# A linear-attention layer followed by a gated long convolution on one core: an order of 1,088 words laid anew

## The chip, the cores and the metric

The kernel runs on one core of a Trainium2 chip. The metric is the device time of one execution in microseconds; the runs of the kernel before took 159.25, 159.96 and 160.06 us, median 159.96. One further execution was profiled. A core has five engines that work through their own instruction lists: TensorE (PE, matmuls; its weight loads are shown as PEld), VectorE (DVE), ScalarE (ACT), GpSimd (POOL) and SyncE (SP), whose queue (SPq) starts the transfers (DMA).

## The reference

Two layers follow one another, over 4 batches, 8 heads, 768 steps and 48 channels in a head.

```python
state = np.zeros((B, H, D, D))
for t in range(S):
    y[:, :, t] = einsum('bhd,bhde->bhe', r_t, state + einsum('bhd,bhe->bhde', u * k_t, v_t))
    state = w_t[..., None] * state + einsum('bhd,bhe->bhde', k_t, v_t)
x = y laid out as (4, 768, 384)
x1, x2, x3 = split(x @ w_proj, 3)
x2_conv = irfft(rfft(x2, axis=1) * rfft(filter_fft, axis=0), n=768)
out = (x1 * x2_conv * x3) @ w_out
```

The first part is a recurrence with a decay w per step and channel, the second a circular convolution over the whole sequence, with a gate on either side.

## The kernel before, in words

The sequence of each batch is cut into 6 chunks of 128 steps, 24 chunks in all; chunk c belongs to batch c // 6. A chunk needs four loads (ldw, ldk, ldr, ldv, 192 KB each; six buffers of each kind). The logarithm of w (lw, ACT) is summed along the steps by two matmuls with triangular masks (cs with the step itself, ce without it), and exponentials of the sums (eq, en) scale r and k: q on the one side, kh on the other. These products can be made in two forms: ACT writes the exponential to SBUF and POOL multiplies (en and kh, eq and q), or ACT writes it back into its PSUM bank and DVE multiplies from there (enp and khp, eqp and qp). TensorE transposes both (tqk), a copy brings them back (tT, L231 or L232), their products are the scores (sc), and DVE masks them while it copies them from PSUM (mt, L560); in another form ACT copies (ma) and POOL masks (mm). Keys and values give the state (kv, then S on DVE, L589). The step's own term, with u, is a product rk of r and k, times u (rku), summed per head (cc) and multiplied onto v (vc); it is added either by a matmul with the identity in the word yb, after which a copy takes the result (xc), or by DVE (y, then xn). The chunk's output is transposed (yt) into xT, and the second half of a batch also makes sums and differences with the first half (sa, sb).

When these exist, the second layer of that batch can start: projections x2 (L682) of sums and differences, copied by ab; the forward transform f (L395, L402) with a matrix F of sines; products with the filter's transform T in the tables UA, UB and their sum P (da, db or X, ua, ub; pp); projections p1 and p3 (L651) with copies x1 and the gate g (or gc by ACT and gm); the inverse transforms i1, i2 (L722), a copy ec, sums and differences s and d (L744, L753), the gate product yy, the output matmul po (L764), its copy o and the store st. Batches overlap: chunks 6 to 11 are worked on while batch 0 is in its second layer.

At the start the kernel also makes its constants. POOL writes a ramp into the first row block of the tile filt (iota), DVE makes 384-wide angles from it (ang0 to ang2, L316, and one column, angn), and ACT takes the sines that are F, and the twelve factors rot (sin, L332 and L336, which needs another ACT table than the logarithms and exponentials; the table is changed back at its end, L337). The filter's load ldfilt (L346, 1,152 KB) overwrites the ramp, so it waits for the angle words. From the filter fs makes the sum of its two halves (L385) and fd the difference (L388); hf0 to hf5 transform them, and rot, which rsc scales (L340), weighs the results into T (ht on ACT, L420, and hr on DVE, L425). The transposed blocks of F for the inverse are mtr, mc and ms. The words z and zs are matmuls of zeros on TensorE whose result nobody reads, 512 or 128 columns wide, as many as the number behind the name says (L791, L796).

The order is written out in one string, ORDER, of 1,088 words. A word such as `P:hf0@3` names the engine (P TensorE, V VectorE, A ScalarE, G GpSimd, S SyncE), the operation with its arguments, and behind the @ the PSUM bank. Every engine works through its own words in the order of the string; semaphores follow from the data and from buffers that are used again. A word with an exclamation mark takes its turn: it also waits for the last VectorE word before it in the string whose operation stands in the set `shut`, as emit arranges it:

```python
if e == "V" and op in shut:
    last[0] = ins
if after and ins is not None and last[0] is not None:
    tc.add_manual_dep(ins.ins, last[0].ins.name, ...)
```

Here ins is what the operation's function returns, and some of these functions return nothing.

## Time and profile before

| what | value |
|---|---|
| runs | 159.25, 159.96, 160.06 us |
| the profiled execution | 159.13 us |
| its span, first to last instruction | 157.4 us |
| PE, DVE, ACT, POOL busy | 142.6, 136.6, 126.0, 111.0 us |
| mean granted TensorE clock | 0.966 |
| read from and written to HBM | 22.61 and 4.72 MB |

The span is the part of the device time that the profile sees. Busy times of matmuls are modelled from their starts, so a busy TensorE need not be at its peak. In a timeline row stand the start and the duration in us, the engine, the line of the kernel, the operation, output and inputs, and in brackets how long the engine was idle before, and for whom.

### The profile page before, as it was taken

The numbers are of one execution on the slowest core, as the hardware profiler recorded it, in microseconds if no ns is written. First come the engines' busy times: TensorE is split into PE (matmuls) and PEld (weight loads), VectorE is DVE, ScalarE is ACT, GpSimd is POOL, SyncE is SP. The second block draws the span as 40 slices with busy tenths as digits, with TensorE's granted clock in tenths as the row PEclk, the third lists the DMA queues.
The fourth block names the chain that finished last, engine by engine and source line by source line (L and its number), as shares of the span: only waits on it lengthen the run. The fifth ranks groups of instructions, "written<-read, shape, count | busy, mean of one in ns | idle before, by whom it ended". The sixth has DMA issues, their size and how long they took to land.

```text
span 157.4 us, 4146 instructions
## 1 busy us (share of the span) xinstructions
PE 142.6 (91%) x1541; PEld 92.8 (59%) x1544; DVE 136.6 (87%) x264; ACT 126.0 (80%) x261; POOL 111.0 (71%) x134
## 2 busy tenths in 40 slices
PE   6972499899899999999899999999999999999970
PEld 6441266667565667676566667676666767545530
DVE  5425978999999999999999989999999999998940
ACT  3795439999898999999898999999897887655541
POOL 7121728999999959899939994789699939283000
PEclk9997559999999999999999999999999999999999
DMA  5998989999996989999999899999945000000966
GB/s 102 203 277 184 215 170 201 209 251 191 236 210 145 265 160 213 186 203 218 179 252 189 158 205 196 187 226 216 218 138 200 0 4 2 0 0 4 329 240 233
DMA packets 105844, 27.60 MB, mean 175 GB/s; under 512 B 100320, under 2 KB 105824, under 8 KB 105824
## 3 DMA queue, kind: packets, MB, share of 16 engines
q1 hardware_dynamic: 105824, 27.34, 77.4%
q8 instruction: 12, 0.20, 0.5%
q14 instruction: 8, 0.07, 0.1%
HBM read 22.61 MB, written 4.72 MB: 174 GB/s over the span
## 4 chain that ended last, share of the span: by engine, by line
PE 58%; ACT 10%; DVE 8%; DMA 8%; POOL 5%; issue 5%; SPq 3%; ACTq 0%; DVEq 0%; POOLq 0%
PE p L651 13%; PE x L682 6%; PE po L764 6%; DMA ldk<-in_k_dram 5%; PE f L402 5%; PE tqk L540 4%; PE i L722 4%; PE sc L553 3%; PE f L395 3%; SPq L450 2%; DMA ldw<-in_w_dram 2%; PE y L606 2%; PE ce L466 2%; DVE rot L340 2%; ACT xT L231 2%
## 5 line engine op out<-in xcount | busy, mean ns | idle before, releaser
L651 PE MATMUL p<-xT,wproj 128*128 128x384 bf16 x144 | 29.0, 326 | 0.0
L521 POOL TENSOR_TENSOR rk<-ldr,ldk 128x384 bf16<-128x384 f32 x23 | 23.0, 1002 | 7.4 <-DMA ldk<-in_k_dram 3.1
L560 DVE TENSOR_TENSOR mt<-sc,mask_excl 128x1024 bf16<-128x1024 f32 x22 | 26.7, 1216 | 0.5 <-PE sc L553 0.4
L231 ACT ACTIVATE qkT<-tqk 128x1024 bf16<-128x1024 bf16 x21 | 21.6, 1027 | 2.4 <-PE tqk L540 1.7
L534 POOL TENSOR_TENSOR vc<-v,cc 128x384 bf16<-128x384 bf16 x24 | 19.8, 831 | 3.8 <-ACT v L231 1.5
L518 POOL TENSOR_TENSOR qk<-ldr,eq 128x384 bf16<-128x384 f32 x17 | 17.0, 1001 | 3.0 <-ACT eq L485 3.0
L651 PEld LDWEIGHTS <-wproj 128*128 128x128 bf16 x144 | 12.8, 98 | 7.3 <-DVE sd L641 0.3
L540 PE MATMUL tqk<-ident,qk 128*128 128x128 bf16 x192 | 15.4, 223 | 1.1 <-DVE qk L502 1.1
L682 PE MATMUL x<-wproj,sd 128*128 128x384 bf16 x72 | 15.0, 326 | 1.0 <-ACT ab L231 0.6
L524 POOL TENSOR_TENSOR rku<-rk,u_bc 128x384 bf16<-128x384 bf16 x15 | 13.7, 915 | 2.7 <-DVE y L756 1.5
L722 PE MATMUL i<-m_b,P 128*128 128x384 bf16 x72 | 15.0, 326 | 0.0
L764 PE MATMUL po<-wout,y 128*128 128x384 bf16 x72 | 14.5, 326 | 0.5 <-DVE y L756 0.3
L540 PEld LDWEIGHTS <-qk 128*128 128x128 bf16 x192 | 12.1, 99 | 4.6 <-DVE qk L502 1.7
L456 ACT ACTIVATE lg<-ldw 128x384 bf16<-128x384 f32 x24 | 12.6, 524 | 2.5 <-DMA ldw<-in_w_dram 2.5
L514 POOL TENSOR_TENSOR qk<-ldk,en 128x384 bf16<-128x384 f32 x12 | 12.0, 1002 | 2.4 <-ACT x L231 2.0
L231 ACT ACTIVATE ab<-x 128x384 bf16<-128x384 f32 x24 | 11.4, 495 | 2.5 <-PE x L682 2.3
L527 DVE TENSOR_REDUCE cc<-rku 128x8 f32<-128x384 bf16 x24 | 12.9, 541 | 0.0
L231 ACT ACTIVATE x<-p 128x384 bf16<-128x384 f32 x24 | 11.6, 501 | 0.7 <-PE p L651 0.7
L231 ACT ACTIVATE xT<-yt 128x384 bf16<-128x384 bf16 x23 | 11.0, 494 | 1.0 <-DVE sd L638 0.8
L589 DVE TENSOR_TENSOR S<-kv,eq 128x384 bf16<-128x384 f32 x20 | 11.0, 550 | 0.8 <-PE kv L581 0.7
L710 DVE TENSOR_TENSOR UA<-f,T 128x768 bf16<-128x768 f32 x11 | 10.4, 949 | 0.3 <-PE f L395 0.3
L677 POOL TENSOR_TENSOR g<-g,x 128x384 bf16<-128x384 bf16 x8 | 7.2, 913 | 4.7 <-DVE g L677 2.6
(137 smaller groups left out, 372.8 us busy)
## 6 DMA issues: line engine op xcount, KB each, us to landing
ldw<-in_w_dram SPq DMA_DIRECT2D x24, 192.0 KB, 3.7
ldr<-in_r_dram SPq DMA_DIRECT2D x24, 192.0 KB, 3.9
ldk<-in_k_dram SPq DMA_DIRECT2D x24, 192.0 KB, 3.9
ldv<-in_v_dram SPq DMA_DIRECT2D x24, 192.0 KB, 4.0
out_dram<-o SPq DMA_DIRECT2D x12, 192.0 KB, 2.2
out_dram<-filt SPq DMA_DIRECT2D x12, 192.0 KB, 2.1
...
filt<-in_moe_filter_fft_dram SPq DMA_DIRECT2D x1, 1152.0 KB, 8.4
```

The costliest lines, as they stand in the source:

```text
L231: return nc.scalar.activation(out=o, in_=i, func=AF.Copy)
L518: return two(e).tensor_mul(qk_b[c % 3][:, 0, :, 0:D], ld["r"][c % LD], eq)
L521: return two(e).tensor_mul(rk_b[c % 2], ld["r"][c % LD], ld["k"][c % LD])
L524: return two(e).tensor_mul(rku_b[c % 2], rk_b[c % 2], u_bc)
L527: nc.vector.tensor_reduce(out=cc_b[c % 3], in_=rku_b[c % 2], axis=AX.X, op=ALU.add)
L534: return two(e).tensor_mul(vc_b[c % 3], v_b[c % 4], cc_b[c % 3].to_broadcast([L, H, D]))
L540: nc.tensor.transpose(p[:, x, j, :], qk_b[c % 3][:, x, 2 * j:2 * j + 2, :], ident)
L560: nc.vector.tensor_mul(mt_b[c % 3], bank_of[f"sc{c}"].rearrange("p q j t -> p (q j) t"), dataclasses.replace(m[:, :], ap=[m[:, :].ap[0], [ ...
L651: nc.tensor.matmul(p, wproj[:, n, cb, fb * L:(fb + 1) * L], xT_b[b % 2][:, cb, sl], start=(cb == 0), stop=(cb == CB - 1),)
L682: nc.tensor.matmul(p, sd_b[q][:, cb, ti * L:(ti + 1) * L], wproj[:, 1, cb, :], start=(cb == 0), stop=(cb == CB - 1),)
L722: nc.tensor.matmul(p, P_b[b % 2][:, s // 2, s % 2, cb * L:(cb + 1) * L], m_b[:, s].rearrange("p a t -> p (a t)"), start=(i == 0), stop=(i ...
L764: nc.tensor.matmul(p, y_b[0][:, cb, ti * L:(ti + 1) * L], wout[:, cb, :], start=(cb == FIRST[0]), stop=(cb == FIRST[-1]),)
```

## The change

The string ORDER is written anew: 1,077 words instead of 1,088, nearly all at other places. What is computed stays as it was. The first line of it before and now:

```diff
-S:ldw0 V:mem0 G:iorot! G:mke! G:iota! P:zs29@0 A:tLn S:ldw2 A:lw0 S:ldw1 S:ldr0 G:mki! S:ldk0 A:lw2
+S:ldw0 A:tLn V:mem2 V:mem4 G:iota! V:ang1 S:ldw1 G:iorot! G:mke! S:ldk0 V:ang0 V:ang2 G:mkd! V:mem0
...
     shut = {"kh", "q", "rk", "rku", "vc", "v", "ua", "ub", "pp", "yy", "gm", "wc",
-            "fs", "fd", "hb", "ang", "angn", "he", "uc"}
+            "fs", "fd", "hb", "ang", "angn", "he", "uc", "rsc"}
```

The word rsc is now in `shut`; its function, op_rsc, returns nothing, so after it the last turn is empty, and POOL words with the mark wait for no turn until DVE has a new one.

Words that change engine or form, as counts before and now:

| operation | before | now |
|---|---|---|
| z, zs on PE | 6 words (18 matmuls), 8 (46) | none, 3 (32) |
| bonus matmul: yb, y | 9, 15 | 6, 18 |
| fd; cast of u (uc) | POOL; POOL | DVE; ACT |
| kh on POOL, khp on DVE | 12, 12 | 18, 6 |
| mt on DVE; ma with mm | 22; 2 | 20; 4 |
| g on DVE; gc on ACT | 12; 12 | 16; 8 |
| rku on POOL, DVE | 15, 9 | 12, 12 |
| rk on POOL, DVE | 23, 1 | 21, 3 |
| pp on POOL, DVE | 3, 9 | 1, 11 |
| xn on DVE; xc on ACT, DVE | 15; 8, 1 | 18; 6, 0 |
| mc on DVE, ACT | 3, 0 | 0, 3 |

Two places are shown from DVE's list and one from ACT's. First DVE's small words at its very start, before and now; o is the tile that holds the angles, filt the ramp, lg, offs, ones and warm are constants.

```order
L300 MEMSET offs 1x4
L293 MEMSET ones 128x2
L316 TENSOR_SCALAR o_165<-filt,tcol 128x384 x2
L288 MEMSET lg_103 128x8x8
L288 MEMSET lg_104 128x8x8
L288 MEMSET lg_105 128x8x8
L316 TENSOR_SCALAR o_165<-filt,tcol 128x384 x4
L323 TENSOR_SCALAR o_165<-tcol 128x3
```

DVE's list at the same place in the changed kernel:

```order
L298 MEMSET offs 1x4
L314 TENSOR_SCALAR o_165<-filt,tcol 128x384 x6
L283 MEMSET warm 128x256
L286 MEMSET lg_103 128x8x8
L286 MEMSET lg_104 128x8x8
L286 MEMSET lg_105 128x8x8
L321 TENSOR_SCALAR o_165<-tcol 128x3
L291 MEMSET ones 128x2
```

All six angle words now stand ahead of the memsets of warm (mem0), lg (mem1) and ones (mem3). On POOL the ramp's words now also stand first.

Second, DVE around the filter: UA<-filt is fs (and now also fd), rot is rsc, qk<-cs is khp, rk and rku are the products of the step's own term, cc its sum, T is hr.

```order
L524 TENSOR_TENSOR rku_117<-rk_115,u_bc 128x384
L502 TENSOR_TENSOR qk_106<-cs_262,ldk_85 128x8x48
L518 TENSOR_TENSOR qk_106<-ldr_91,eq_112 128x8x48
L385 TENSOR_TENSOR UA<-filt 128x1152
L306 MEMSET sgn 64x1
L307 MEMSET sgn 64x1
L340 TENSOR_TENSOR rot<-rot,rsc 128x12
L527 TENSOR_REDUCE cc_123<-rku_117 128x8
L502 TENSOR_TENSOR qk_108<-cs_326,ldk_87 128x8x48
L502 TENSOR_TENSOR qk_107<-cs_319,ldk_86 128x8x48
```

DVE around the filter in the changed kernel, where the rows that write rsc only set its constants:

```order
L383 TENSOR_TENSOR UA<-filt 128x1152
L300 MEMSET rsc 128x12
L301 MEMSET rsc 1x3
L302 MEMSET rsc 1x1
L386 TENSOR_TENSOR UA<-filt 128x1152
L338 TENSOR_TENSOR rot<-rot,rsc 128x12
L500 TENSOR_TENSOR qk_106<-cs_298,ldk_85 128x8x48
L519 TENSOR_TENSOR rk_115<-ldr_91,ldk_85 128x384
L522 TENSOR_TENSOR rku_117<-rk_115,u_bc 128x384
L519 TENSOR_TENSOR rk_116<-ldr_92,ldk_86 128x384
L522 TENSOR_TENSOR rku_118<-rk_116,u_bc 128x384
L423 SCALAR_TENSOR_TENSOR T<-hf_315,rot,E_155 128x384
```

Before, chunk 0's products rku, khp and q stand ahead of fs; now fs, fd and rsc stand ahead of khp0, rk0 and rku0. q0 has gone to POOL.

Third, ACT from its start: lg is lw, cs<-cs is enp, eq the other exponential, F and rot are the sines, E is ht, u_bc the cast of u.

```order
L328 ACT_TABLE_LOAD
L456 ACTIVATE lg_103<-ldw_79 128x8x48
L456 ACTIVATE lg_105<-ldw_81 128x8x48
L456 ACTIVATE lg_104<-ldw_80 128x8x48
L492 ACTIVATE cs_262<-cs_262 128x384
L485 ACTIVATE eq_112<-ce_264 128x392
L332 ACT_TABLE_LOAD
L332 ACTIVATE F<-o_165 128x768 x3
L336 ACTIVATE rot<-rang 128x12
L337 ACT_TABLE_LOAD
L492 ACTIVATE cs_326<-cs_326 128x384
```

ACT from its start in the changed kernel:

```order
L326 ACT_TABLE_LOAD
L330 ACT_TABLE_LOAD
L330 ACTIVATE F<-o_165 128x768 x3
L334 ACTIVATE rot<-rang 128x12
L335 ACT_TABLE_LOAD
L454 ACTIVATE lg_104<-ldw_80 128x8x48
L454 ACTIVATE lg_103<-ldw_79 128x8x48
L229 ACTIVATE u_bc<-u_all 128x384
L454 ACTIVATE lg_105<-ldw_81 128x8x48
L483 ACTIVATE eq_112<-ce_284 128x392
L490 ACTIVATE cs_298<-cs_298 128x384
L418 ACTIVATE E_155<-hf_305,rot 128x384
```

The sines stand ahead of the first logarithms now, and the logarithm of chunk 2's w ahead of chunk 0's exponentials. On SP the first transfers are now w0, w1, k0, u, filter, w2, r0, k1; before they were w0, w2, w1, r0, k0, u, filter, k2, k1.

More of the change, by code (lines that the diff above doesn't have):

```diff
@@ L37 @@
 ORDER = """
-S:ldw0 V:mem0 G:iorot! G:mke! G:iota! P:zs29@0 A:tLn S:ldw2 A:lw0 S:ldw1 S:ldr0 G:mki! S:ldk0 A:lw2
-S:ldu V:mem2 V:mem4 V:mem3 V:ang1 V:mem1 V:ang2 V:ang0 A:lw1 V:angn P:cs0@0 P:ce0@1 P:z3@2 P:z7@3
-A:enp0 P:ce1@2 S:ldfilt A:eq0 P:zs1@3 G:mkd! G:rk0! G:uc! S:ldk2 P:zs8@1 V:mem5 V:rku0 V:khp0 P:z2@3
-P:cs1@1 A:sin P:cs2@4 P:z1@3 V:q0 S:ldk1 P:zs1@5 V:fs S:ldv0 A:enp2 A:ph1 A:enp1 P:zs2@3 P:zs2@5
-P:tqk0@5 V:mem6 G:fd! P:hf0@3 V:rsc V:cc0 V:khp2 P:mtr0@0 P:hf1@4 A:tT0 A:ht0.0 P:ce2@5 P:sc0@8
@@ L126 @@
[L126 to L128 removed]
+S:ldw0 A:tLn V:mem2 V:mem4 G:iota! V:ang1 S:ldw1 G:iorot! G:mke! S:ldk0 V:ang0 V:ang2 G:mkd! V:mem0
+G:mki! V:mem1 S:ldu S:ldfilt S:ldw2 V:angn P:zs29@0 A:sin V:mem3 A:lw1 A:lw0 P:ce1@0 V:fs V:mem5
+A:uc S:ldr0 A:lw2 P:ce0@1 V:fd S:ldk1 P:mtr2@2 P:cs0@3 V:rsc A:eq0 A:enp0 G:q0! V:khp0 P:hf0@4 V:rk0
@@ new lines @@
+V:rku0 S:ldr1 A:ht0.0 P:cs2@1 P:hf1@5 P:ce2@3 A:eq1 S:ldr2 A:ms2 V:rk1 A:ht0.1 S:ldv0 A:en2 P:cs1@0
+V:rku1 V:hr0.0 A:en1 G:kh1! A:v0 S:ldw3 P:tqk0@4 S:ldk2 P:hf2@0 P:mtr0@1 V:tT0 A:eq2 V:hr0.1 A:he
+A:lw3 V:cc1 S:ldv1 A:ht1.1 A:ht1.0 P:sc0@8 A:mc0 A:v1 P:kv0@4 V:mt0 P:zs2@5 V:S0 V:mem6 A:mc2 V:ms0
+P:zs1@3 P:ce3@3 P:hf4@5 G:q2! G:q1! P:tqk1@0 P:hf3@4 V:cc0 P:cs3@1 G:rk2! G:kh2! V:hr1.0 G:vc1!
+S:ldr3 S:ldw4 P:kv1@2 V:S1 A:eq3 A:tT1 A:lw4 V:rku2 S:ldw5 V:q3 S:ldk3 V:hr1.1 P:sc1@8 V:mt1 V:cc2
+P:ce4@0 P:cs4@2 A:ht2.0 P:hf5@3 A:lw5 S:ldk4 S:ldr4 G:rk3! G:vc0! S:ldw6 P:y0@4 A:en3 A:eq4 A:ht2.1
```

166 lines of the change are left out of this document (80 added, 86 removed).

## The prediction

> **What bounds the kernel now.** First the page: the busy shares, the granted clock, the chain that ended last.
>
> ```profile
> span 157.4 us, 4146 instructions
> PE 142.6 (91%) x1541; PEld 92.8 (59%) x1544; DVE 136.6 (87%) x264; ACT 126.0 (80%) x261; POOL 111.0 (71%) x134
> ...
> PE 58%; ACT 10%; DVE 8%; DMA 8%; POOL 5%; issue 5%; SPq 3%; ACTq 0%; DVEq 0%; POOLq 0%
> ```
>
> TensorE leads, but four engines are full. So the second view is the busy time by stages, with the clock.
>
> ```profile
> 13.68:17.09 3.41, 1.55 (x7) 0.86 (x7) 3.13 (x4) 0.14 (x1) 1.78 (x1) 0.50 0.89 170
> 17.09:20.50 3.41, 1.58 (x13) 0.89 (x14) 2.93 (x6) 2.25 (x5) 1.92 (x3) 0.50 1.11 222
> 20.50:23.92 3.42, 3.42 (x32) 2.15 (x34) 2.94 (x6) 1.17 (x3) 0.82 (x2) 0.50 0.72 144
> 24.00:40.00 16.00, 14.69 (x219) 10.46 (x220) 15.51 (x29) 15.69 (x33) 15.08 (x18) 1.00 1.03 218
> 40.00:148.70 108.70, 107.72 (x1183) 70.15 (x1180) 104.30 (x190) 93.19 (x199) 86.48 (x94) 1.00 0.73 160
> ```
>
> Columns: PE, PEld, DVE, ACT, POOL, clock, DMA share, GB/s. From 40 to 148.7 us TensorE is busy 107.72 of 108.70 us and DVE 104.30: hardly a microsecond is to be had there, unless work goes. From 24 to 40 DVE and ACT are full. Slack lies before 24 us, so the third view is the order of time there, on the engines that wait for the filter. DVE first:
>
> ```profile
> 3.00 0.78 DVE L316 TENSOR_SCALAR o<-filt,tcol 128x384 int32<-128x384 f32 x2 [0.50 <-POOL filt L265]
> ...
> 3.93 1.36 DVE L316 TENSOR_SCALAR o<-filt,tcol 128x384 int32<-128x384 f32 x4
> ...
> 13.87 1.36 DVE L385 TENSOR_TENSOR UA<-filt 128x1152 bf16<-128x1152 f32 x1 [1.74 <-DMA filt<-in_moe_filter_fft_dram]
> ...
> 15.38 2.56 DVE L340 TENSOR_TENSOR rot<-rot,rsc 128x12 f32<-128x12 f32 x1
> 17.87 0.54 DVE L527 TENSOR_REDUCE cc<-rku 128x8 f32<-128x384 bf16 x1
> 18.33 1.00 DVE L502 TENSOR_TENSOR qk<-cs,ldk 128x384 bf16<-128x384 f32 x2
> ...
> 22.66 1.21 DVE L560 TENSOR_TENSOR mt<-sc,mask_excl 128x1024 bf16<-128x1024 f32 x1
> ```
>
> Then POOL, ACT, the DMA queue, the landing time of the filter, and TensorE:
>
> ```profile
> 0.90 0.15 POOL L269 IOTA rang<- 128x8 f32 x1 [0.39 <-POOLq L848]
> ...
> 1.91 0.14 POOL L259 IOTA tcol<- 128x3 f32 x1
> ...
> 2.73 0.24 POOL L265 IOTA filt<- 128x128 f32 x1
> ...
> 15.31 2.61 POOL L388 TENSOR_TENSOR UA<-filt 128x1152 bf16<-128x1152 f32 x1 [4.51 <-DVE UA L385]
> ```
>
> ```profile
> 3.74 0.52 ACT L456 ACTIVATE lg<-ldw 128x384 bf16<-128x384 f32 x1 [1.66 <-DMA ldw<-in_w_dram]
> ...
> 6.42 0.48 ACT L485 ACTIVATE eq<-ce 128x392 f32<-128x392 f32 x1
> 6.92 1.28 ACT L332 ACT_TABLE_LOAD   x1
> 8.21 2.31 ACT L332 ACTIVATE F<-o 128x768 bf16<-128x768 int16 x3
> 10.43 0.20 ACT L336 ACTIVATE rot<-rang 128x12 f32<-128x12 f32 x1
> ...
> 18.04 0.58 ACT L420 ACTIVATE E<-hf,rot 128x384 f32<-128x384 f32 x1 [4.22 <-DVE rot L340]
> ```
>
> ```profile
> 5.44 0.37 SPq L346 DMA_DIRECT2D filt<-in_moe_filter_fft_dram  x1
> 5.85 1.63 SPq L450 DMA_DIRECT2D ldk<-in_k_dram  x2
> 7.53 6.16 SPq L450 DMA_DIRECT2D ldv<-in_v_dram  x1
> ```
>
> ```profile
> filt<-in_moe_filter_fft_dram SPq DMA_DIRECT2D x1, 1152.0 KB, 8.4
> ```
>
> ```profile
> 15.28 1.12 PE L402 MATMUL hf<-UA,F 128*128 128x384 bf16 x3 [2.70 <-DVE UA L385]
> ...
> 20.41 0.61 PE L553 MATMUL sc<-qkT 48*128 48x128 bf16 x8
> ```
>
> The filter is issued at 5.44 us, because its load overwrites the ramp that the angle words read (the last ends at 5.29), and DVE starts on it at 13.87. The sum fs ends at 15.2; the difference fd then runs on POOL for 2.61 us; rsc, twelve elements wide, lasts 2.56 us beside it. ACT's first E word waits 4.22 us for rsc; sc0 runs at 20.41, and chunk 0's first mask product mt0 at 22.66. Until then the filter is the bound.
>
> **The start, step by step.** The filter is issued when the angle words end. POOL now makes the ramp first. In the rows tcol starts at 1.91 and the ramp ends at 2.97, 1.06 us; from POOL's first word, 0.90, that is 1.96. DVE's small words in front now end at 2.50 (3.00 less 0.50 idle); mem0 and mem3 have left them, so about 2.1. Six angle words (0.78 + 1.36 us) then end at 4.25. The issue moves from 5.44 to about 4.35: 1.1 us. Two loads fewer (w2, r0) stand ahead of it; two go behind it, as k2 and k1 do now. At the 215 or so GB/s that the stage rows show, 0.39 MB are 1.8 us, but bytes behind it share the engines. The gain in landing is at least 0 (a full queue), at most 2.9; I take 1.7, from the issue and a third of the bytes: landing at 12.2.
>
> fs then ends at 13.5 and fd, now on DVE at the 1.36 us of fs, at 14.9; rsc follows, 0.1 us, between nothing and the 0.20 that ACT takes for the same twelve elements: 15.0, against 17.94 now. That is 1.7 of landing and 1.25 of fd, 2.95 in all. One thing can take some of it: q0 on POOL carries the turn mark, yet rsc has just cleared it (its function returns nothing). If q0 gets in between fd and rsc, rsc waits out about one POOL word of 1.0 us, as it waits out fd now. In the Trainium skill, "SBUF — State Buffer", section "SBUF: two separate sides", the port pair of the two engines is an exclusive lock held for a whole instruction; the two rows at 15.3 agree, 2.56 beside 2.61. I count half: 0.5.
>
> ACT pays for this. The sine words now come first; they wait for angn (behind three memsets, about 4.9), run 2.31 + 0.20 us, and the table that follows takes 1.28: 8.7. So lw1 and lw0 start there instead of 3.74. Then lw2 stands ahead of eq0, and w2 was issued behind the filter and lands about 12.7, so eq0 ends near 13.6, not 6.9, with enp0 behind it. What hides this is the filter: DVE's khp0 stands behind fd and rsc and starts at 15.0 anyway. Without that cover it would cost the 6.7 us. hf0 runs from 13.5 to 14.6 (1.12). The scaled copies ht0.0 and ht0.1, with eq1 and ms2 between them, are four ACT words of 0.4 to 0.5 and end at 16.7 to 17.2; tqk0 reuses their bank and follows, eight matmuls like sc0's 0.61; then hf2 (like hf0) and mtr0 stand ahead of sc0, which also needs the copy tT0 (DVE, 0.6). That is mt0 at 19.4 to 20.3, say 19.9. DVE's own words from rsc to there (khp0, two rk, two rku, two hr, tT0, cc1: about 4 us) fit. So mt0 comes 2.8 us sooner than 22.66.
>
> **The cast of u** goes from POOL to ACT, which only waits for w2 then: nothing; uncovered it is 0.4. **The zero words** are dropped where TensorE waits for the filter or DVE: nothing; their cost through the clock is a rival below.
>
> **The long stretch.** DVE's list behind mt0 is the measure, since DVE is full from 24 to 40 and 104.30 of 108.70 after. Starts stand 0.09 closer than ends (17.87 to 18.33 for 0.54), so I take means less 0.09.
>
> ```profile
> L560 DVE TENSOR_TENSOR mt<-sc,mask_excl 128x1024 bf16<-128x1024 f32 x22 | 26.7, 1216 | 0.5 <-PE sc L553 0.4
> L534 POOL TENSOR_TENSOR vc<-v,cc 128x384 bf16<-128x384 bf16 x24 | 19.8, 831 | 3.8 <-ACT v L231 1.5 <-ACT E L231 1.1 <-DVE rku L524 0.7
> L710 DVE TENSOR_TENSOR UA<-f,T 128x768 bf16<-128x768 f32 x11 | 10.4, 949 | 0.3 <-PE f L395 0.3
> L716 DVE TENSOR_TENSOR P<-UA,UB 128x768 bf16<-128x768 bf16 x9 | 4.6, 553 | 0.1
> L638 DVE TENSOR_TENSOR sd<-xT,yt 128x384 bf16<-128x384 bf16 x12 | 4.1, 350 | 0.4 <-ACT eq L485 0.2
> L232 DVE COPY qkT<-tqk 128x1024 bf16<-128x1024 bf16 x3 | 2.1, 686 | 0.0
> ```
>
> Behind mt0 it loses two mt (2 x 1.13), one da (0.86) and one tT (0.6). Of 384-element words with a float operand (0.46), four khp, one xc and one o go, and three xn, four g and one qp come: two more, +0.92. Of 768-wide bf16 words (0.46), ua, ub and two pp come and one yy goes: +1.4. Of small bf16 words (0.26) two rku and one xT come, mc and gm go: +0.26. A vc comes, which DVE has not run: between 0.26 and POOL's 0.83, I take 0.4, nearer to bf16 on DVE. Sum: -3.72 + 2.98 = -0.7. TensorE drops three bonus matmuls, a gain I leave out. POOL's list gets shorter (pp, gm, fd, rku less, six kh more), and it was not the bound; ACT takes two ma, a wc and three mc and gives away gc, and has 15.5 us of room after 40 (108.70 - 93.19).
>
> New waits in a new order have no row. Bounds: DVE is idle 0.49 + 4.40 us between 24 and 148.7; if half of that went, 2.4 us better; if it doubled, 4.9 worse. A list this full has more to lose, so I put 0.5 against the change. The end is built as before: nothing.
>
> **Sum.** 2.8 + 0.7 - 0.5 = 3.0 us, so the span falls from 157.4 to 154.4. The profiled execution took 159.13 for its span of 157.4, 1.7 around it, which gives 156.1; from the median of the three runs, 159.96, it is 157.0. I forecast the middle, 156.6.
>
> **The rivals.** *The loads set the pace.* The DMA share is 1.03 from 24 to 40, and SP's load of v0 was stuck 6.16 us. If transfers, not DVE, pace the first chunks, only the landing gain of 1.7 stays, less 0.8 (1.63 for two) for a transfer more that now stands ahead of v5: 0.9, so 158.7. Against it: after 14 us no engine in the wait lists waits for a load long.
>
> *The lead is eaten.* DVE's idle time after 24 us goes up by 3 us, because words of other engines come late: 159.6. For it: every engine is nearly full; against it: nothing in the counts.
>
> *The clock stays at half, and the kernel is slower.* The rows show 0.50 until 23.92 though zero words ran early, and full speed only after a stage in which TensorE was busy 3.42 of 3.42; so much is now dropped that it may stay cold. Work between the filter and the first x2 word is at most 14.69 plus half of 1.55 + 1.58 + 3.42, 18.0 us at full speed, in the 24.5 us from 13.5 to 38. A cold stretch c loses c/2; past the 6.5 us of room and the lead of 3.0 it costs: the point is c = 19, a clock that returns after 32.5 us. If it returns at 40, 13.25 - 9.5 = 3.7 slower than before: 163. Against it stand the zero words' own rows, short ones and long ones, in slices of 3.93 us:
>
> ```profile
> busy tenths in 40 slices 9490000010000000000000000000000000000000
> ```
>
> ```profile
> busy tenths in 40 slices 0950002220000000000000000000000000000000
> ```
>
> Between 11.8 and 23.6 us none ran, and yet the clock came back; cold matmuls fill their time by being slow, and hf0 to sc0 now fill 13.5 to 19 nearly without a gap. The Trainium skill, "TensorE: Matmul & The Clock Gate", section "Part 1: The HAM clock gate", states that about 3.4 us of sustained work release the clock and an idle window of that length takes it back. The trace agrees with the release: one full 3.42 us stage, then 1.00. By that rule the clock is back near 17 to 20 us even without zeros; mt0 would come at the early end, 19.4, and the sum be 156.1.
>
> **How the numbers follow.** Forecast 0.60; loads 0.13; eaten 0.14; cold 0.09; waits that shrink by the 2.4 bound, 153.6 to 154.2, 0.04. Within 0.5% means 159.2 to 160.8, about what a measurement can tell. Faster takes nearly all of the first, most of the second, the last: 0.74; same 0.12; slower 0.14. The range runs from 153.6, the shrunken waits with a landing gain of 2.3, to 160.6, past the eaten lead; the cold clock is left out.
>
> **What would show it.** Right: fs starts at 11.6 to 12.8; rsc ends 2.8 us later; mt0 near 19.9; mt5, now at 40.10, near 37.5 to 38.5; the clock at 1.00 by 21; DVE still over 94% busy after 40.
>
> ```profile
> 40.10 1.22 DVE L560 TENSOR_TENSOR mt<-sc,mask_excl 128x1024 bf16<-128x1024 f32 x1
> ```
>
> Wrong: fs still near 13.9; eq0 later than fd, so that khp0 waits; an mt5 that is early while the last matmul is not; a clock of 0.50 past 30.

## The result, and the profile after

The kernel after takes 158.51 us (median of 20 runs, 157.36 to 159.88). The kernel before, run beside it, takes 159.66 (20 runs, 158.37 to 160.37). The ratio is 0.9932, 95% interval 0.9911 to 0.9953: 1.1 us faster, where 3.0 were forecast. The sign was right and the size was not. Here and below the ratios leave out runs over 1.5% above the fastest of their kernel (two of the kernel after, one each of zeros_back, zeros_and_turn and new_two_loads_less), and the medians do not. The profiled execution took 158.28 us, with a span of 156.5; before it was 159.13 and 157.4, so the two traces lie 0.9 us apart in their spans, a little less than the medians.

Line numbers of the kernel after are two lower than before (the mask product L560 is now L558). The page of the kernel after, its span, busy shares and chain:

```profile
span 156.5 us, 4070 instructions
...
PE 137.3 (88%) x1506; PEld 91.0 (58%) x1506; DVE 134.6 (86%) x265; ACT 129.0 (82%) x265; POOL 105.3 (67%) x129
...
PE 49%; DVE 30%; issue 6%; ACT 4%; DMA 4%; POOL 3%; ACTq 0%; POOLq 0%; DVEq 0%
```

TensorE has lost 5.3 us of busy time (142.6 to 137.3), though its zeros alone lost 6.9 (10.7 to 3.8), and the chain now runs over VectorE for 30% of the span instead of 8%. Neither says where the time went. So first the start, on DVE, from the filter's sum fs (L383) and difference fd (L386) over rsc (L338) to the mask products of chunks 0, 1 and 5 (mt0, mt1, mt5):

```profile
11.23 1.36 DVE L383 TENSOR_TENSOR UA<-filt 128x1152 bf16<-128x1152 f32 x1 [6.42 <-DMA filt<-in_moe_filter_fft_dram]
...
12.67 1.35 DVE L386 TENSOR_TENSOR UA<-filt 128x1152 bf16<-128x1152 f32 x1
...
13.94 0.96 DVE L338 TENSOR_TENSOR rot<-rot,rsc 128x12 f32<-128x12 f32 x1
...
20.17 1.23 DVE L558 TENSOR_TENSOR mt<-sc,mask_excl 128x1024 bf16<-128x1024 f32 x1 [0.57 <-PE sc L551]
...
24.00 0.62 DVE L423 SCALAR_TENSOR_TENSOR T<-hf,rot,E 128x384 bf16<-128x384 f32 x1 [1.17 <-PE hf L393]
...
26.33 1.22 DVE L558 TENSOR_TENSOR mt<-sc,mask_excl 128x1024 bf16<-128x1024 f32 x1
...
38.96 1.21 DVE L558 TENSOR_TENSOR mt<-sc,mask_excl 128x1024 bf16<-128x1024 f32 x1
...
148.44 0.56 DVE L754 TENSOR_TENSOR y<-SD,g 128x768 bf16<-128x768 bf16 x1
```

mt0 is 2.49 us earlier than before (20.17 against 22.66). mt1 is only 0.83 earlier (26.33 against 27.16), and mt5 1.14 (38.96 against 40.10). mt1 in the kernel before:

```profile
27.16 1.21 DVE L560 TENSOR_TENSOR mt<-sc,mask_excl 128x1024 bf16<-128x1024 f32 x1
```

Twice DVE now waits for TensorE, 0.57 us ahead of mt0 and 1.17 ahead of the turn at 24.00. The last row is the last gate product, which ends at 149.00. The same word of the kernel before:

```profile
150.36 0.56 DVE L756 TENSOR_TENSOR y<-SD,g 128x768 bf16<-128x768 bf16 x1
```

It ended at 150.92, so 1.92 us of lead arrive there. What was won and lost between mt0 and that word is read from DVE's busy time, first in the kernel before, then in the kernel after (columns as in the stages of the prediction; the third is DVE):

```profile
22.66:24.00 1.34, 1.34 (x16) 1.20 (x18) 1.23 (x3) 1.25 (x3) 0.20 (x1) 0.53 0.21 41
...
40.00:150.92 110.92, 109.53 (x1191) 70.84 (x1188) 106.41 (x194) 94.20 (x201) 86.48 (x94) 1.00 0.73 163
```

```profile
20.17:24.00 3.83, 3.77 (x31) 2.27 (x30) 2.57 (x7) 3.05 (x7) 3.09 (x4) 1.00 0.84 164
24.00:40.00 16.00, 12.53 (x207) 9.54 (x206) 15.97 (x28) 15.06 (x32) 13.42 (x16) 1.00 0.97 203
40.00:149.00 109.00, 107.35 (x1173) 70.67 (x1172) 103.97 (x195) 95.23 (x200) 80.87 (x88) 1.00 0.75 164
```

Before, with the 15.51 us from 24 to 40 that the prediction shows, DVE has 1.23 + 15.51 + 106.41 = 123.15 us of work in 128.26 us. After, it has 2.57 + 15.97 + 103.97 = 122.51 us in 128.83 (149.00 less 20.17). So the work fell by 0.64 us, and the idle time rose from 5.11 to 6.32, by 1.21. Nearly all of that rise lies before 24 us: 3.83 less 2.57 is 1.26, against 0.11 before. Behind 24 us the idle time is 5.06 us against 5.00.

The last step is the end. The six stores of the last batch, issued by SP, in the kernel before and in the kernel after:

```profile
151.86 2.79 SPq L784 DMA_DIRECT2D out_dram<-filt  x6
```

```profile
149.95 2.84 SPq L782 DMA_DIRECT2D out_dram<-filt  x6
```

They start 1.91 us earlier and the span ends 0.9 earlier. The missing microsecond shows in what the DMA engines do from 153 to 157 us, in slices of 0.1 us, before and after:

```profile
GB/s 369 369 369 369 338 384 399 354 323 399 323 430 338 384 323 415 353 399 323 384 323 415 353 400 323 399 338 399 338 139 0 0 0 0 0 0 0 0 0 0
```

```profile
GB/s 384 353 399 338 400 338 384 353 415 338 169 62 61 15 31 15 31 0 0 0 0 0 0 0 0 0 0 0 0 0 0 0 0 0 0 82 0 0 0 0
...
q14 instruction: 1, 0.01, 0.7%
```

Before, data run at about 370 GB/s up to the last slice with traffic, 155.9 to 156.0; the last packet ends at 156.06, 1.32 us ahead of the span's end. After, the rate falls at 154.0 and a thin rest of 15 to 62 GB/s trails until 154.73, 1.75 us ahead of the end. At 156.53, just behind the span's end, stands one more transfer of 8 KB: a load of instructions. The lead in the stores' data is thus 1.3 us, and 0.9 at the end. The account of the two profiled executions:

| step | forecast | measured |
|---|---|---|
| first mask product | 2.8 | 2.49 |
| less work for VectorE behind it | 0.7 | 0.64 |
| more idle time of VectorE behind it | -0.5 | -1.21 |
| from the last gate product to the span's end | 0 | -1.03 |
| sum | 3.0 | 0.89 |

### The profile page after: what moved, and what is told of

It reads as the page before. It is cut to its first block, busy times and chain, and to the rows that moved or that the text cites. A ratio compares the mean times of both kernels' runs of the same rounds, so it can differ in the third digit from the quotient of the medians.

```text
span 156.5 us, 4070 instructions
## 1 busy us (share of the span) xinstructions
PE 137.3 (88%) x1506; PEld 91.0 (58%) x1506; DVE 134.6 (86%) x265; ACT 129.0 (82%) x265; POOL 105.3 (67%) x129
## 4 chain that ended last, share of the span: by engine, by line
PE 49%; DVE 30%; issue 6%; ACT 4%; DMA 4%; POOL 3%; ACTq 0%; POOLq 0%; DVEq 0%
PE p L649 9%; PE x L680 6%; DVE mt L558 5%; PE i L720 5%; DMA filt<-in_moe_filter_fft_dram 4%; PE tqk L538 4%; PE po L762 4%; PE f L400 4%; DVE g L665 3%; DVE xn L616 3%; DVE cc L525 3%; PE sc L551 3%; PE f L393 2%; DVE S L587 2%; DVE UA L708 2%
## 5 line engine op out<-in xcount | busy, mean ns | idle before, releaser
L516 POOL TENSOR_TENSOR qk<-ldr,eq 128x384 bf16<-128x384 f32 x18 | 18.7, 1041 | 14.1 <-ACT eq L483 8.3
L558 DVE TENSOR_TENSOR mt<-sc,mask_excl 128x1024 bf16<-128x1024 f32 x20 | 24.3, 1215 | 0.6 <-PE sc L551 0.6
L519 POOL TENSOR_TENSOR rk<-ldr,ldk 128x384 bf16<-128x384 f32 x21 | 21.0, 1001 | 3.9 <-DVE qk L516 2.7
L512 POOL TENSOR_TENSOR qk<-ldk,en 128x384 bf16<-128x384 f32 x18 | 18.0, 999 | 5.2 <-DVE T L423 2.8
L532 POOL TENSOR_TENSOR vc<-v,cc 128x384 bf16<-128x384 bf16 x23 | 18.9, 830 | 2.4 <-DVE rku L522 1.8
L538 PEld LDWEIGHTS <-qk 128*128 128x128 bf16 x192 | 12.8, 102 | 4.1 <-issue 1.3
L720 PE MATMUL i<-m_b,P 128*128 128x384 bf16 x72 | 14.5, 326 | 0.0
L522 POOL TENSOR_TENSOR rku<-rk,u_bc 128x384 bf16<-128x384 bf16 x12 | 10.9, 912 | 2.1 <-DVE y L754 2.1
L616 DVE TENSOR_TENSOR xn<-y,vc 128x384 bf16<-128x384 f32 x18 | 9.9, 553 | 1.3 <-PE y L604 1.0
L711 DVE TENSOR_TENSOR UB<-f,T 128x768 bf16<-128x768 f32 x11 | 10.3, 950 | 0.2 <-PE f L393 0.2
```

The lines of the kernel that those rows point to most:

```text
L512: return two(e).tensor_mul(qk_b[c % 3][:, 1, :, 0:D], ld["k"][c % LD], en_b[c % 3])
L516: return two(e).tensor_mul(qk_b[c % 3][:, 0, :, 0:D], ld["r"][c % LD], eq)
L519: return two(e).tensor_mul(rk_b[c % 2], ld["r"][c % LD], ld["k"][c % LD])
L532: return two(e).tensor_mul(vc_b[c % 3], v_b[c % 4], cc_b[c % 3].to_broadcast([L, H, D]))
L538: nc.tensor.transpose(p[:, x, j, :], qk_b[c % 3][:, x, 2 * j:2 * j + 2, :], ident)
L558: nc.vector.tensor_mul(mt_b[c % 3], bank_of[f"sc{c}"].rearrange("p q j t -> p (q j) t"), dataclasses.replace(m[:, :], ap=[m[:, :].ap[0], [ ...
```

## The experiments

Twelve kernels. "mt0" and "mt5" are the starts of these words; "stores" is the issue of the first store of the last run of stores on SP; "rest" is the time from the stores' last packet to the span's end; all in us, from the one profiled execution of each.

| kernel | median | ratio to before, interval | span | mt0 | mt5 | stores | rest |
|---|---|---|---|---|---|---|---|
| before | 159.66 | | 157.4 | 22.66 | 40.10 | 151.86 | 1.32 |
| after | 158.51 | 0.9932, 0.9911 to 0.9953 | 156.5 | 20.17 | 38.96 | 149.95 | 1.75 |
| zeros_back | 157.80 | 0.9902, 0.9881 to 0.9922 | 156.7 | 19.77 | 38.19 | 150.56 | 1.71 |
| rsc_turn | 157.86 | 0.9904, 0.9869 to 0.9940 | 157.4 | 19.34 | 38.42 | 151.24 | 1.75 |
| zeros_and_turn | 157.97 | 0.9895, 0.9850 to 0.9940 | 156.6 | 19.27 | 38.38 | 150.48 | 1.72 |
| zeros_turn_two_loads_less | 156.87 | 0.9862, 0.9826 to 0.9897 | 155.2 | 19.33 | 37.80 | 149.03 | 1.87 |
| new_two_loads_less | 158.60 | 0.9932, 0.9899 to 0.9964 | 156.2 | 20.29 | 38.03 | 149.82 | 1.93 |
| fd_on_pool | 158.68 | 0.9965, 0.9938 to 0.9991 | 156.9 | 21.02 | 38.83 | 150.47 | 1.37 |
| filter_late | 157.78 | 0.9899, 0.9871 to 0.9927 | 155.6 | 19.57 | 37.74 | 149.30 | 1.75 |
| filter_late_pool_pad | 157.53 | 0.9888, 0.9854 to 0.9921 | 155.2 | 20.14 | 38.12 | 149.10 | 1.30 |
| old_no_zeros | 160.32 | 1.0049, 1.0025 to 1.0074 | 158.5 | 23.02 | 40.25 | 152.19 | 1.29 |
| old_fd_vector | 158.32 | 0.9925, 0.9895 to 0.9955 | 156.6 | 21.59 | 39.54 | 151.04 | 1.31 |
| new_four_stores_less | 156.98 | 0.9865, 0.9834 to 0.9896 | 155.4 | 20.64 | 39.08 | 151.59 | 1.80 |
| old_four_stores_less | 159.12 | 1.0001, 0.9982 to 1.0020 | 157.2 | 22.40 | 40.17 | 153.77 | 1.42 |

The theory after the comparison of the two traces had two parts: TensorE at half pace behind mt0 takes back 1.2 us, and the stores at the end take back 1.0. The rivals: the loads hold everything, or the lead never was worth what the order suggests.

**zeros_back: zeros ahead of the first inputs, in the new order.** Four words, 20 matmuls of 512 columns (only the parts of the lines that change are shown, here and below):

```diff
-G:mki! V:mem1 S:ldu S:ldfilt S:ldw2 V:angn P:zs29@0 A:sin
+G:mki! V:mem1 S:ldu S:ldfilt S:ldw2 V:angn P:zs29@0 P:z6@8 A:sin
-P:mtr2@2 P:cs0@3 V:rsc
+P:mtr2@2 P:cs0@3 P:z4@8 V:rsc
-P:hf1@5 P:ce2@3
+P:hf1@5 P:z6@8 P:ce2@3
-S:ldw3 P:tqk0@4
+S:ldw3 P:z4@8 P:tqk0@4
```

> The changed kernel with 20 zero matmuls of 512 columns put into TensorE's waits before the filter's transform (6 ahead of ce1, 4 ahead of hf0, 6 ahead of ce2, 4 ahead of tqk0). Theory A, the lead was lost to a TensorE at half pace: the stretch from tqk0 (16.87 us) to hf3 (23.9 us), all TensorE in the chain of the changed kernel, runs at full pace; sc0's eight matmuls take 0.40 us instead of 0.61, the wait of 1.17 us ahead of hr1.0 (24.00) goes, mt1 starts near 24.5 instead of 26.33, and the time falls by 1 to 2 us against the changed kernel, to a ratio of about 0.982 to 0.987 to before. Rival B, DVE and ACT set the pace there and only the waits move: mt1 within 0.5 us, ratio 0.992 to 0.994. Rival C, the zeros delay hf0 and the rest: slower, ratio above 0.995.

Measured 0.9902: between the first theory's forecast and the second's, and its interval overlaps that of the kernel after a little. The trace shows both halves of the answer. First TensorE from 16 to 24 us in the kernel after, two of its words, and then the same in zeros_back:

```profile
16.00:24.00 8.00, 7.56 (x59) 4.35 (x58) 5.83 (x14) 6.77 (x16) 5.61 (x6) 1.00 0.99 192
```

```profile
16.87 1.01 PE L538 MATMUL tqk<-ident,qk 128*128 128x128 bf16 x8 [0.37 <-ACT E L418]
...
22.26 1.06 PE L538 MATMUL tqk<-ident,qk 128*128 128x128 bf16 x8
```

```profile
16.00:24.00 8.00, 6.84 (x81) 4.11 (x80) 7.57 (x18) 7.79 (x19) 5.62 (x6) 1.00 0.97 191
```

```profile
17.53 0.61 PE L538 MATMUL tqk<-ident,qk 128*128 128x128 bf16 x8
...
21.36 0.61 PE L538 MATMUL tqk<-ident,qk 128*128 128x128 bf16 x8
```

The eight transposes of tqk take 1.01 and 1.06 us in the kernel after and 0.61 with the zeros, and TensorE does 81 matmuls in less busy time than 59 took. mt1 then starts at 24.95 instead of 26.33. So between these two executions the half pace cost 1.4 us at mt1; that part of the theory holds. But at mt5 only 0.8 of it is left (38.19 against 38.96), and the stores start later than in the kernel after. What stands between is a wait that the kernel after doesn't have, on ACT and then on PE:

```profile
66.04 0.52 ACT L454 ACTIVATE lg<-ldw 128x384 bf16<-128x384 f32 x1 [1.05 <-DMA ldw<-in_w_dram]
```

```profile
67.38 0.32 PE L458 MATMUL cs<-lg,mask_incl 128*128 128x384 bf16 x1 [0.83 <-ACT eq L483]
```

A load of w lands too late, ACT stands 1.05 us, TensorE 0.83. That was a new theory: behind a start that is earlier still, the loads set the pace.

**rsc_turn: rsc becomes a partner of the turns**, so that GpSimd's q0 waits until it is done:

```diff
     def op_rsc(e, k_):
-        nc.vector.tensor_mul(rot, rot, rsc)
+        return nc.vector.tensor_mul(rot, rot, rsc)
```

> The changed kernel with op_rsc returning its instruction, so that q0 on POOL takes its turn behind rsc. If q0 between fd and rsc is what makes rsc last 0.96 us (13.94 to 14.90), rsc takes under 0.2 us, ht0.0 starts near 14.2 instead of 15.00 and mt0 near 19.5 instead of 20.17; if such a lead passes through to the end, 0.5 to 0.8 us are gained, ratio about 0.988 to 0.990. Rival: q0, now later, is what tqk0 waits for, or the half-pace TensorE takes it all back: ratio 0.992 to 0.994, mt0 within 0.2 us.

Measured 0.9904, with an interval that holds both forecasts. In the trace the mechanism is plain. GpSimd's q0 in the kernel after, and rsc and q0 in rsc_turn:

```profile
13.14 1.73 POOL L516 TENSOR_TENSOR qk<-ldr,eq 128x384 bf16<-128x384 f32 x1 [8.35 <-ACT eq L483]
```

```profile
14.35 0.16 DVE L338 TENSOR_TENSOR rot<-rot,rsc 128x12 f32<-128x12 f32 x1
```

```profile
14.65 1.00 POOL L516 TENSOR_TENSOR qk<-ldr,eq 128x384 bf16<-128x384 f32 x1 [9.86 <-DVE rot L338]
```

In the kernel after q0 runs 1.73 us beside fd and ends at 14.87, and rsc beside it lasts 0.96 and ends at 14.90; apart they last 1.00 and 0.16. That fits the exclusive lock on the port pair that the Trainium skill describes in "SBUF — State Buffer", section "SBUF: two separate sides". The prediction took 0.5 us for this collision; it is 0.8. In this execution TensorE was also at full pace from 16.0 us on by the clock's record, and mt5 came at 38.42. Then ACT waited 0.82 us for a load of v at 67.8 us and TensorE 0.67 at 69.3: the same loss at the same place as in zeros_back. Both executions took longer than the median of their kernel (158.39 against 157.80, 159.07 against 157.86), so the wait need not stand in every one.

**zeros_and_turn**, the two diffs above together:

> The kernel after with both earlier edits: four words with 20 more matmuls of zeros ahead of the first inputs, and the angles' product as a partner of the turns. Each of them by itself brought the sixth masking 0.5 to 0.8 us forward (38.96 to 38.19 and 38.42) and then showed a wait that the kernel after does not have: at 65 to 70 us ScalarE waited 1.05 us for a load of w, or 0.82 us for a load of v, and TensorE stood 0.83 and 0.67 us. Theory A (loads bind as soon as the start is over 1.5 us earlier): sixth masking near 37.5 to 38.2, the wait at 65 to 70 us at least as long, and no more gain than with one edit: ratio 0.988 to 0.992. Theory B (leads pass through to the end): the gains add, ratio 0.983 to 0.987.

Measured 0.9895: the gains do not add, and the ratio is theory A's. Its signs came in part: mt5 at 38.38 lies just behind the 37.5 to 38.2, and the waits, 0.86 us of ACT for w and 0.64 of TensorE at 66.7 us, are no longer than those of zeros_back.

**zeros_turn_two_loads_less** leaves out two loads of 576 KB, so that the second and third weights are cast from what the buffer holds:

```diff
-P:sc8@8 S:ldp2
+P:sc8@8
-A:lw13 S:ldp3
+A:lw13
```

> The kernel with both edits, and without the loads of the third of the projection's weights and of the output weights (576 KB each; their casts read what the first third left in the buffer, so the output is not the reference's). One of the two loads stood at 49.8 us, ahead of the wait at 65 to 70 us, and takes about 2.8 us of the DMA engines at the 200 to 210 GB/s of that stretch. Theory A (loads bind there): the wait at 65 to 70 us is gone and the time is 0.7 to 1.5 us below that of the kernel with both edits: ratio 0.979 to 0.985. Theory B (the wait has another reason): within 0.3 us of the kernel with both edits.

Measured 0.9862, behind theory A's range: 0.5 us below zeros_and_turn by the ratios, 1.1 in the medians. The intervals overlap, so the trace has to decide. TensorE, DVE and ACT from 60 to 76 us, in zeros_and_turn and without the two loads:

```profile
60.00:76.00 16.00, 14.52 (x181) 9.97 (x180) 14.74 (x32) 12.98 (x28) 14.86 (x17) 1.00 1.02 202
```

```profile
60.00:76.00 16.00, 15.16 (x186) 10.44 (x185) 15.44 (x33) 13.81 (x30) 14.28 (x16) 1.00 1.00 197
```

TensorE gains 0.64 us there, DVE 0.70, ACT 0.83; no wait for a load is left there, and the last stores start at 149.03 instead of 150.48. So the loads did bind in the execution of zeros_and_turn.

**new_two_loads_less**, the same two words S:ldp2 and S:ldp3 left out of the kernel after itself:

> The kernel after without the loads of the third of the projection's weights and of the output weights (their casts read what the first third left in the buffer, so the output is not the reference's). With zeros and turn the same omission took away a wait at 65 to 70 us and the time fell by 1.1 us. Theory A (the loads bind only where the start is further ahead than in the kernel after, which shows no such wait on TensorE or VectorE): within 0.4 us of the kernel after, ratio 0.990 to 0.994. Theory B (the DMA engines, busy all the time up to 112 us, hold the kernel after back as well): 0.8 to 1.5 us faster than the kernel after, ratio 0.983 to 0.988.

Measured 0.9932, the ratio of the kernel after: theory A. In the kernel after as it stands the loads are not what holds it. This run shows one more thing. Up to 49 us its words are those of the kernel after, and yet the same word, hf4, three matmuls, reads so in the kernel after and here:

```profile
21.34 1.12 PE L400 MATMUL hf<-UA,F 128*128 128x384 bf16 x3
```

```profile
21.32 0.65 PE L400 MATMUL hf<-UA,F 128*128 128x384 bf16 x3
```

The half pace ended near 21.3 us here and near 23 there, and mt1 came at 25.40 against 26.33. So when the half pace ends differs from one execution to the next by about 2 us, and with it mt1 by 0.9: the 1.2 us of idle time in the account are those of one execution.

That lead of 0.9 us reaches the last copy out of PSUM whole (150.53 against 151.45), yet the last six stores begin only 0.13 earlier. Three other stores stand ahead of them, in the kernel after and here:

```profile
147.76 1.31 SPq L782 DMA_DIRECT2D out_dram<-o  x3
```

```profile
146.83 2.89 SPq L782 DMA_DIRECT2D out_dram<-o  x3
```

The third of them takes 2.03 us to issue instead of 0.45. So it does, with 1.88 to 2.17 us, in four of the ten traces of the new order (rsc_turn, fd_on_pool and new_four_stores_less are the others) and in none of the four of the old; why isn't known. It held the six stores back by 0.8 us here.

**old_no_zeros: the eleven zero words out of the old order**, nothing else (zs29@0, zs2@0 and zs1@0 stay). By their numbers they are 21 matmuls of 512 columns, of which the trace before has 18 records, and 14 of 128:

```diff
-P:cs0@0 P:ce0@1 P:z3@2 P:z7@3
+P:cs0@0 P:ce0@1
...
-A:enp0 P:ce1@2 S:ldfilt A:eq0 P:zs1@3 G:mkd! G:rk0! G:uc! S:ldk2 P:zs8@1 V:mem5 V:rku0 V:khp0 P:z2@3
-P:cs1@1 A:sin P:cs2@4 P:z1@3 V:q0 S:ldk1 P:zs1@5 V:fs S:ldv0 A:enp2 A:ph1 A:enp1 P:zs2@3 P:zs2@5
+A:enp0 P:ce1@2 S:ldfilt A:eq0 G:mkd! G:rk0! G:uc! S:ldk2 V:mem5 V:rku0 V:khp0
+P:cs1@1 A:sin P:cs2@4 V:q0 S:ldk1 V:fs S:ldv0 A:enp2 A:ph1 A:enp1
...
-P:sc1@8 P:z3@4 G:rk3!
+P:sc1@8 G:rk3!
...
-A:eq4 P:z5@4 V:ms1
+A:eq4 V:ms1
```

> The kernel before without the eleven zero words that the new order lacks, all else as before. The zero words did not keep the clock from falling at 13.68 us in the run shown. Theory A': they bought nothing, since TensorE is at half pace from 13.68 to 23.92 us with them too; without them it starts cold and is at half pace until it has been busy long enough, about 23 to 24 us: ratio 0.998 to 1.002. Rival: they do matter behind 24 us, where four words stand between the chunks, and the clock falls or comes late: ratio 1.005 to 1.03. Other rival: they stood in the way and cost time themselves: ratio 0.99 to 0.997.

Measured 1.0049: the zeros were worth 0.5% in the old order, against the forecast of nothing and just short of the first rival's range. How isn't shown by the trace. mt0 is 0.36 us later, but so is fs (14.22 against 13.87); at mt5 0.15 are left, and the last copy out of PSUM is 0.33 later. The rest of this span's 1.1 us lies in the last stores, which take 5.03 us from their first issue to their last packet instead of 4.20.

**fd_on_pool: fd back on GpSimd in the new order:**

```diff
-A:uc S:ldr0 A:lw2 P:ce0@1 V:fd S:ldk1
+A:uc S:ldr0 A:lw2 P:ce0@1 G:fd! S:ldk1
```

> The changed kernel with the filter's difference fd back on POOL, all else as changed. The prediction priced the move to DVE at 1.25 us: with the difference on POOL rsc should last about 2.5 us beside it and end near 15.2 to 15.4, against 14.90 now that q0 already takes 0.9 of the gain; q0 comes after fd on POOL, near 15.2 to 16.2, and tqk0 at 16.9 to 17.3. So the price against the changed kernel should be 0.3 to 0.5 us, ratio 0.995 to 0.997; rival: the full 1.25 us shows at the end, ratio 1.000 to 1.001; or nothing, 0.993, if TensorE's half pace behind it hides it.

Measured 0.9965, the ratio of its first forecast: rsc lasts 2.47 us again beside fd's 2.61, and mt0 is 0.85 us later than in the kernel after. The time is some 0.5 us longer by the ratios; the intervals overlap. Its trace doesn't show that the 0.85 us came through: TensorE was at full pace from 22.0 us by the clock's record, against 23.3 in the kernel after, and from mt1 on (26.20 against 26.33) to the last copy out of PSUM (151.32 against 151.45) this execution is even 0.13 us ahead. What makes its span longer are the stores: the one with the long issue, 1.88 us, and the data of the last six.

**old_fd_vector: fd on VectorE in the old order**, one word:

```diff
-P:tqk0@5 V:mem6 G:fd! P:hf0@3 V:rsc V:cc0
+P:tqk0@5 V:mem6 V:fd P:hf0@3 V:rsc V:cc0
```

> The kernel before with only the filter's difference on VectorE, in place of GpSimd. In the kernel before the difference (2.61 us on GpSimd) and the angles' product (2.56 us on VectorE) ran at the same time, 15.3 to 17.9 us; on VectorE the difference takes 1.35 and the product 0.1 to 0.2 us, so that both end at 16.7 to 16.9 us. Theory A: 1.0 us of lead at the product, 0.6 to 1.0 at the first masking, ratio 0.994 to 0.997. Theory B (the half pace of TensorE up to 23.9 us and VectorE's list behind it take the lead): same as the kernel before, 0.998 to 1.001.

Measured 0.9925, theory A and more: this one word gives 1.2 us, as much as the whole change. DVE and the last stores in its trace:

```profile
15.45 1.36 DVE L388 TENSOR_TENSOR UA<-filt 128x1152 bf16<-128x1152 f32 x1
16.72 0.16 DVE L340 TENSOR_TENSOR rot<-rot,rsc 128x12 f32<-128x12 f32 x1
```

```profile
151.04 2.80 SPq L784 DMA_DIRECT2D out_dram<-filt  x6
```

rsc ends at 16.88 instead of 17.94. Of these 1.06 us, 1.07 are left at mt0, 0.56 at mt5, 0.82 at the first of the last stores and 0.8 at the span's end, with 1.31 us behind the last packet as in the kernel before. In the old order a lead of about 1 us goes through to the end almost whole.

**filter_late: two loads back ahead of the filter's load**, in the new order:

```diff
-S:ldu S:ldfilt S:ldw2 V:angn
+S:ldu S:ldw2 S:ldr0 S:ldfilt V:angn
-A:uc S:ldr0 A:lw2
+A:uc A:lw2
```

> The kernel after with two loads of 192 KB (w of chunk 2, r of chunk 0) put ahead of the filter's load again, as in the kernel before; nothing else differs. The filter's sums then start near 13 us instead of 11.2, and the first masking comes at 21.5 to 22.5 us instead of 20.2. Theory A (the start's lead is most of the gain and goes through to the first copy out of PSUM): the last batch's first store 1.3 to 2 us later than in the kernel after, ratio to the kernel before 0.998 to 1.004. Theory B (TensorE's half pace up to 23 us or the loads behind 40 us would have taken such a lead anyway): the later start is made good by then, ratio 0.992 to 0.996.

Measured 0.9899: theory B, and beyond it. The filter comes later and the kernel is no slower than the kernel after, if anything faster (the intervals overlap a little). Its trace, DVE and then GpSimd's q0:

```profile
12.48 1.36 DVE L383 TENSOR_TENSOR UA<-filt 128x1152 bf16<-128x1152 f32 x1 [7.53 <-DMA filt<-in_moe_filter_fft_dram]
...
15.19 0.16 DVE L338 TENSOR_TENSOR rot<-rot,rsc 128x12 f32<-128x12 f32 x1
...
19.57 1.21 DVE L558 TENSOR_TENSOR mt<-sc,mask_excl 128x1024 bf16<-128x1024 f32 x1
```

```profile
10.95 0.99 POOL L516 TENSOR_TENSOR qk<-ldr,eq 128x384 bf16<-128x384 f32 x1 [6.36 <-ACT eq L483]
```

fs starts 1.25 us later than in the kernel after, but w2 and r0 land earlier (8.01 and 8.70 us instead of 12.12 and 12.99), q0 is done at 11.94, before fs, and rsc lasts 0.16 us. It ends at 15.35, 0.45 later than in the kernel after. From there to mt0 it is 4.22 us instead of 5.27, since TensorE was at full pace from 16.9 us by the clock's record in this execution; why so early is open. The filter's earlier landing, the largest term of the forecast, is worth nothing that can be measured here: rsc_turn, with the filter first and q0 out of rsc's way, ends rsc 0.84 us sooner (14.51) and has no better ratio, 0.9904.

**new_four_stores_less and old_four_stores_less.** Both leave out the same four of the last six stores:

```diff
-P:pob3.3 P:pob3.4 S:st3.5 A:o3.0 V:o3.3 S:st3.1 S:st3.0 A:o3.2 S:st3.2 A:o3.4 S:st3.4 S:st3.3
+P:pob3.3 P:pob3.4 A:o3.0 V:o3.3 A:o3.2 A:o3.4 S:st3.4 S:st3.3
```

That is the new order; in the old one the words S:st3.5, S:st3.0, S:st3.2 and S:st3.1 go in the same way.

> The kernel after without the last batch's stores of rows 5, 0, 2 and 1 (those four blocks of the output are left out; the two stores issued last stay). In the profiled run of the kernel after, the last copy out of PSUM ended at 151.45 us, 2.6 us before that of the kernel before, yet the span ended only 0.9 us before. Theory (the stores' tail gives the lead back: six stores of 192 KB move in about 3.2 us from the first copy on, whenever the last copy comes): with two stores left the end follows the last copy, the two issues behind it and one landing: span near 155.0, ratio to the kernel before 0.980 to 0.986. Rival (the tail is the same in both and the lead was lost elsewhere): it falls as much as the kernel before does with the same four stores left out, so that 1.0 to 1.3 us stay between the two.

> The kernel before without the same four stores (four blocks of the output left out). There the last copy out of PSUM ended at 154.06 us and the last store was issued 0.6 us later, so that the stores hardly trail it. Theory: 0.1 to 0.6 us faster than the kernel before, ratio 0.996 to 0.999, and 2.0 to 2.6 us between this kernel and the one after with four stores less. Rival: it gains as much as the kernel after does (1 us or more), and the distance stays 1.0 to 1.3 us.

Measured 0.9865 and 1.0001, each just above its range. The kernel before gains nothing, the kernel after 1.1 us by the ratios, and 2.1 us lie between the two (156.98 against 159.12) instead of 1.1. So the compute part of the new order is some 2 us faster, and about half of that is given back in the last stores. The rows show how. The last copies out of PSUM by ACT, before and after (DVE makes the sixth in between):

```profile
152.81 1.25 ACT L231 ACTIVATE filt<-po 128x384 f32<-128x384 f32 x3 [0.59 <-PE po L764]
```

```profile
149.43 2.02 ACT L229 ACTIVATE filt<-po 128x384 f32<-128x384 f32 x5 [1.70 <-PE po L762]
```

In both orders six stores, issued over 2.8 us, move 1.18 MB at about 370 GB/s, 3.2 us, from the first copy on, so that the end follows the first copy. In the old order the last copies end so late (154.06 us) that they cover this; in the new one they end at 151.45, 2.6 us earlier, the first store goes out only 1.91 earlier, and the stores trail alone. Without four of them the last packets are 2.17 us apart (153.64 against 155.81).

**filter_late_pool_pad: two memsets more on GpSimd**, of a spare tile, just ahead of its last word:

```diff
-P:i23.0@2 P:i23.2@5 G:gm3.2.1!
+P:i23.0@2 P:i23.2@5 G:pad G:pad G:gm3.2.1!
+    def op_pad(e, k_):
+        nc.gpsimd.memset(spare, 0.0)
```

> The kernel with the filter's load behind two others (0.9899 of the kernel before), with two memsets of a spare 128 by 2 tile more on GpSimd, just ahead of its last product. In the profiles of the kernels with the new order the span ends 1.71 to 1.93 us after the last data of the stores, in those with the old order 1.29 to 1.32; the one exception is the new order with the filter's difference on GpSimd, one instruction more there, with 1.37. In the kernels with the longer end, an 8 KB load of instructions starts just after the span's end (156.53 us in the kernel after, 155.70 in this kernel's base); with the one GpSimd instruction more, all loads of instructions are over before the stores end. Theory A (at the end an engine waits for its next instructions, and which engine's list crosses a block's end there hangs on its count): with the two memsets no load of instructions starts at the span's end, 1.3 to 1.4 us lie behind the stores' last data, and the time is 0.3 to 0.5 us lower than without: ratio 0.985 to 0.989. Theory B (the two only coincide): 1.7 us or more lie behind the last data, ratio 0.988 to 0.992.

Measured 0.9888 against 0.9899 for the same kernel without them: 0.25 us in the medians, which the intervals can't tell apart. The trace tells: from 153 to 157 us it now shows no load of instructions,

```profile
GB/s 369 369 200 62 31 15 31 31 15 0 0 0 0 0 0 0 0 0 0 0 0 0 0 0 0 0 0 0 0 0 0 0 0 0 0 0 0 0 0 0
```

the 8 KB block came at 144.28 us instead, and 1.30 us lie between the last packet and the end, as in the old order, instead of 1.75. In all fourteen traces the two go together: with such a load just behind the end 1.71 to 1.93 us (eight traces), without it 1.29 to 1.42 (six). So 0.4 us at the end of the kernel after hang on how many instructions GpSimd has. That an engine waits for instructions there is likely but not shown, since the load itself starts only behind the last instruction. Its median is the lowest of the kernels that compute all of the reference, 157.53 us, but not by more than the intervals. It also shows that an early start need not meet the loads: mt5 came at 38.12, sooner than in zeros_back, and no engine waits for a load from 60 to 76 us.

## Why the prediction came out too large

**The start.** The ramp, the angle words and the issue of the filter went as worked out: issue at 4.38 us, forecast 4.35. The landing was better than taken (6.8 us instead of 8.4; fs at 11.23, forecast 12.2), the collision of q0 and rsc a little worse (0.8 us, forecast 0.5), and TensorE between rsc and mt0 slower (5.27 us, forecast 4.4). mt0 came at 20.17, forecast 19.9: 2.49 us of 2.8, so near because the better landing made good the slower pace, which was luck. But the terms were weighted wrongly, as filter_late and old_fd_vector show. The 1.7 us for the filter's landing are worth nothing measurable, and w2 and r0 behind the filter hold q0 until it meets rsc; the 1.25 us for fd on VectorE are worth 1.2 us by themselves in the old order, and about 0.5 in the new one (fd_on_pool).

**VectorE's list** behind mt0 became 0.64 us shorter, forecast 0.7. DVE was busy 95% after 40 us (103.97 of 109.00), as forecast.

**The reserve for new waits** was the first step that failed: "I put 0.5 against the change". 1.21 us came. The reserve was taken from DVE's idle time behind 24 us, and there it grew by only 0.06. The other 1.15 us lie between mt0 and 24 us, a stretch for which the sum has no term and in which DVE waits for TensorE at half pace. The prediction saw the half pace as a matter of all or nothing, with 32.5 us as the point from which it counts. Its "6.5 us of room" was TensorE's alone; DVE, behind mt0, had no such room. It asked for full pace by 21 us; the durations show half until about 23. By the rule of the Trainium skill that the prediction weighed ("TensorE: Matmul & The Clock Gate", section "Part 1: The HAM clock gate") full pace was due at 17 to 20 us; the executions of the new order without more zeros show it from 16.0 to 23.3. So the loss is not a fixed size: in new_two_loads_less the same words had mt1 0.93 us sooner.

**The end** was the second, and the larger: "The end is built as before: nothing". In the two executions it costs 1.03 us, 0.6 in the stores' data and 0.43 behind them. Over many runs four stores less show it: 2.1 us lie between the two orders without them and 1.1 with them. The words of the end did change: the copies of the last batch come closer together and 2.6 us sooner, and then six stores take their 3.2 us with nothing to cover them. The row of the six issues stood in the trace of the kernel before. How the 1.03 us divide is less sure. The 0.43 hang on GpSimd's list, as filter_late_pool_pad shows. The 0.6 vary: from the first of the six issues to the last packet it takes 4.20 us in the kernel before and 4.78 in the kernel after, but 4.29 to 5.08 in the other traces of the new order with six stores, and 4.21 and 5.03 in those of the old.

**The rivals.** The loads' time, 158.7, was nearest to the result, but by luck, since its reason was wrong for the kernel after: without two loads it is no faster. Loads were waited for only in some kernels with an earlier start, and not in all of those. The eaten lead had the right kind of loss, at 1.2 us instead of 3, and not where it was put. The cold clock cost part of the lead and did not turn the sign.

What stays open: why TensorE reached full pace at such different times, why a store ahead of the last six is sometimes slow to issue, and how much of the medians' 1.1 us each step makes up, since the account is one execution of each kernel.
